# One planner, four edits: when begun projections go on, how value rounds are cut, which head group VectorE's blocks come from, and when a thin value round may start

## The chip, the cores and the metric

The kernel runs on one core of a Trainium2 chip. The metric is device microseconds of that core for one execution, and runs are compared by their median. A core has five engines that the text names as the profile does: TensorE (PE for its matmuls, PEld for its weight loads), VectorE (DVE), ScalarE (ACT), GpSimd (POOL) and SyncE (SP), which here only issues DMAs. Each engine works through its own queue in the order in which the program has it; semaphores tie the queues together.

## The reference

Two attention blocks stand side by side in the output's columns: A, a linear attention, and B, a full softmax attention. Both have S = 2048 rows, D = 512 columns, 32 heads of 16.

```python
# A: x @ wqkv -> q, k, v of 32 heads with 16 columns each
phi = lambda t: jnp.where(t > 0, t + 1, jnp.exp(t)) + 1e-6
pq, pk = phi(q), phi(k)
kv  = jnp.einsum("bhsd,bhse->bhde", pk, v)
z   = jnp.einsum("bhsd->bhd", pk)
num = jnp.einsum("bhqd,bhde->bhqe", pq, kv)
den = jnp.einsum("bhqd,bhd->bhq", pq, z)[..., None] + 1e-6
a   = (num / den) heads joined @ wo
# B: its own x, wqkv, wo
scores = jnp.einsum("bhqd,bhkd->bhqk", q, k) * Dh ** -0.5
p = softmax(scores)
b = einsum("bhqk,bhkd->bhqd", p, v) heads joined @ wo
return jnp.concatenate([a, b], axis=-1)
```

B's cost is its 32 x 2048 x 2048 exponentials.

## The kernel before

**Units and blocks.** B is cut into 32 units: one of four groups of eight heads (Gp), one of four chunks of 512 queries (c), and the even or the odd heads of the group (e_). A unit has 64 blocks: four head groups g (32 rows of the array each) times 16 key tiles j of 128 keys. One block is a matmul "128 keys by 512 queries" from KM and QT into one PSUM bank (`qk`, line 743). 2048 blocks in all.

**Three ways through PSUM.** Of eight banks, five (pS) are ScalarE's, as one slot of three banks and one of two; two (pD) serve VectorE's blocks and, one at a time, every projection and all of A's work; one (pPV) holds the sum of the values.

- ScalarE's blocks: `fill_act_cand` puts three or two score matmuls into the free slot, and line 905 takes the exponential of the whole slot into PT.
- VectorE's blocks: `d_pick` chooses a block for a free pD bank when VectorE's and GpSimd's backlogs are small. Line 839 computes a scaled and shifted integer into DI that, read as float16, is an approximate exponential; two blocks form a group, and line 952 makes two shifted copies of it on GpSimd (DJ). The three tables are used with three weighted copies of V.
- Values: a block of ScalarE's is one matmul with V (17 columns: 16 and a one for the denominator) into its head group's 32 rows of pPV; a block of VectorE's is three. Up to four, one for each head group, stand side by side in a round (line 998). `pv_cand` forms up to two rounds (PVB is 8) of what is ready.

When a unit's 192 or fewer value matmuls are in, VectorE transposes pPV (line 1023), divides (lines 1028 and 1029), and every other unit is transposed back into ON (line 1034). Then pPV is free for the next unit.

**Jobs.** The projections of B (`proj_job`, `v4_job`), all of A (`akv_job`, `akvsum_job`, `aq_job`, `aden_job`, `anum_job`) and the output matmuls (`omm_job`) are jobs with stages: TensorE stages, mostly two halves of the contraction, into one pD bank, then stages on VectorE, ScalarE or a DMA. The bank is taken with the first half and given back after the first read-out.

**The planner.** All instructions are ordered while the program is built: a loop keeps a planned time T for each engine, collects candidates, each with a start, a priority and a duration, and takes among those that could start within 0.03 us of the earliest the one with the lowest priority number. A score fill for ScalarE has 0; later stages of jobs are put into a list by `push` with their job's priority (2 for most, on TensorE); value rounds have 1 when at least 12 value matmuls are outstanding or the unit is at its end, otherwise 4; a block for VectorE alone has 3. Candidates on TensorE that would still run when ScalarE is due for its next fill are left out. Every instruction goes through `Sched.add`, which finds what it must wait for; writes with the same `accum` tag on the same engine don't wait for each other. The order is the planner's, the times are the chip's.

**Filling idle time.** Where the planner leaves TensorE idle for over 0.25 us, `fill_idle` puts in matmuls of zeros (FZ, line 1155): as many as bring TensorE's share of streaming in the last 3.4 us (FW) to 0.7 (FU). `streams` keeps the planned streaming times.

**The lines that the change touches**

```python
        order = sorted(range(4), key=lambda g: (g in used, -len(rem[u][g]), g))
        ...
            if len(rounds[0]) < 4 and not final and len(rd) < 8:
                t_ += PVW
            dur = switch("v") + 0.22 * len(rounds)
        ...
            return t_, dur, run, (1 if out_ >= 12 or final else 4)
```

The first is `choose`, which says which head group's next block is taken: the one with most blocks left. In the second a first round with fewer than four head groups is held back by PVW, 0.5 us, unless eight value matmuls are ready.

Of the kernel before, what the change touches and what calls it, by code (L numbers as in the profile page):

```python
# [21 lines left out]
class Sched:  # L22
# [16 lines left out]
    def add(self, lane, fn, reads=(), writes=(), name="", queue=None,  # L39
            extra_deps=(), accum=None, force_signal=False):  # L40
        if queue is None:
            queue = lane
            assert lane in self.ENGINES, lane
        op = _Op()
        op.idx = len(self.ops)
        op.lane = lane
        op.fn = fn
        op.pos = len(self.lane_ops[lane]) + 1
        op.name = name
        op.queue = queue  # L50
        op.waits = []
        op.sig = force_signal
        op.count = 0
        deps = set(extra_deps)
        for r in reads:
            w = self.last_write.get(r)
            if w is not None:
                deps.add(w)
        for r in writes:
            w = self.last_write.get(r)  # L60
            if w is not None:
                if not (accum is not None and self.acc_tag.get(r) == (lane, accum)):
                    deps.add(w)
            for rd in self.readers.get(r, ()):
                deps.add(rd)
            self.acc_tag[r] = (lane, accum) if accum is not None else None
# [168 lines left out]
def bass_concat_heads__linear_attn_block__softmax_full_mha__prompt_kernel(nc, A_x, A_wqkv, A_wo, B_x, B_wqkv, B_wo, out):  # L235
# [6 lines left out]
    NU = NGP * NC * 2  # L242
# [18 lines left out]
    FU = 0.7  # L261
    LATE = 0.1
    LONE = 0.0
    FW = 3.4
    TRACE = None

# [8 lines left out]
    with es:  # L275
# [160 lines left out]
        class Job:  # L436
# [13 lines left out]
            def stage_done(self, i, end, bk, bi):  # L450
# [6 lines left out]
                if i + 1 < len(self.stages):  # L457
                    eng2, dur, fn = self.stages[i + 1]
                    push(eng2, end if eng2 == eng else vis(eng, end),
                         self.prio if eng2 == "pe" else (0 if eng2 == "act" or (i + 1 <= self.rel and self.bank) else min(self.prio, 2)), dur,  # L460
                         lambda st_, en_, fn=fn: (fn(bk), self.stage_done(i + 1, en_, bk, bi)), getattr(fn, "kind", "f"))
# [241 lines left out]
        pk = ["f"]  # L703

        def switch(kind):
            return 0.0 if pk[0] == kind else 0.1
# [9 lines left out]

        def choose(u, n, used=()):

            got, t0 = [], 0.0
            order = sorted(range(4), key=lambda g: (g in used, -len(rem[u][g]), g))  # L720
            for g in order:
# [64 lines left out]
        def d_pick(at, used):  # L786
# [14 lines left out]
            else:  # L801
                buf = dgroup["buf"]
            ch = choose(u, 1, used)
            if ch is None or not ch[0] or ch[1] > at:
# [3 lines left out]
        def d_take(pk):  # L808
            b, buf, bi = pk
            take([b])  # L810
            dfree[bi] = None
            if not dgroup["open"]:
# [148 lines left out]
        def pv_cand():  # L961
# [20 lines left out]
            while len(rounds) < PVB // 4 and any(byg):  # L982
# [3 lines left out]
                rounds.append(rnd)  # L986
            if len(rounds[0]) < 4 and not final and len(rd) < 8:
                t_ += PVW
            dur = switch("v") + 0.22 * len(rounds)
            def run(st, en):  # L990
                for x in sum(rounds, []):
# [19 lines left out]
                if todo[u] == 0:  # L1011
# [4 lines left out]
                    push("dve", vis("pe", en), -1, 0.63, lambda st_, en_: unit_done(u, en_))  # L1016
            return t_, dur, run, (1 if out_ >= 12 or final else 4)

# [114 lines left out]

        streams = []

        def fill_idle(st, kind):
# [4 lines left out]
            if not gs and bi is None:  # L1141
                return 0
            lo = st - FW
            while streams and streams[0][1] <= lo - 5.0:
                streams.pop(0)
            need = FU * FW - sum(max(0.0, min(y, st) - max(x, lo)) for x, y in streams)
            a += switch("v")
            n = min(int((b - (0.0 if kind == "v" else 0.1) - a) / 0.216), int(need / 0.216 + 0.999))
            if n <= 0:
                return 0  # L1150
            g = gs[0] if gs else 0
            dst = PVb if gs else f32v(DBANK[bi])
# [14 lines left out]
        while True:  # L1167
# [20 lines left out]
            if pc is not None:  # L1188
                opts.append((pc[0], pc[3], "pe", pc[1], pc[2], None, "v"))
            jc = job_cand()  # L1190
# [10 lines left out]
            t0 = min(o[0] for o in opts)  # L1201
            o = min((o for o in opts if o[0] <= t0 + 0.03), key=lambda o: (o[1], o[0]))
            st, _, eng, dur, run_, c_, kind = o
# [101 lines left out]
```

## Time and profile before

| | |
|---|---|
| median of three runs | 765.57 us (763.3 to 768.93) |
| the profiled execution | 767.73 us, its span 765.8 us |
| instructions | 18359 |
| mean granted clock of TensorE | 0.973 |
| HBM read and written | 4.19 MB each, 11 GB/s over the span |

How to read it: a busy time is the union of an engine's instructions, a group's row gives output and inputs by the program's names, the shape, the count, the busy time and the mean of one in ns, and behind the second bar the engine's idle time just before these instructions with what ended it. Line numbers are those of the kernel before.

The stages run into each other, so there are no phases to set apart but the start, some 11.6 us in which inputs land and the first projections are made, and the end, the last 9 us with the last output rows.

```profile
0.81 5.50 DMA xTb<-in_B_x_dram
6.35 1.90 PE pS L476 x16
8.25 2.96 PE pD L476 x31
11.58 46.66 ACT PT L905 x41
```

These are the first pieces of the chain of waits in order of time: start, length, what.

### The profile page before, as it was taken

To read this page: it belongs to the slowest core of one execution; us is meant where nothing else is said; L and a number is where in the kernel's file an instruction comes from. 1 tells how busy PE (TensorE), PEld (TensorE's weight loads), DVE (VectorE), ACT (ScalarE), POOL (GpSimd) and SP (SyncE) were. 2 spreads that over 40 slices of the span, in tenths; PEclk is the share of its full clock that TensorE was granted. 3 is DMA by queue.
4 is the path that set the end of the run, shared out by engine and by line. 5 is a ranking of instruction groups with operands and counts; after the bars stand their busy time and mean duration, and the time that the engine had idled before them with its cause. 6 is when DMAs were issued, how large, how long until landed. Compare 5 with 4: busy or idle time off the path is not lost.

```text
span 765.8 us, 18359 instructions
## 1 busy us (share of the span) xinstructions
PE 696.7 (91%) x7975; PEld 225.5 (29%) x7975; DVE 541.7 (71%) x858; ACT 732.2 (96%) x664; POOL 535.0 (70%) x529
## 2 busy tenths in 40 slices
PE   8899999989899999899999999999998899999886
PEld 4322333333323233322222223322222222222222
DVE  5885868787767767759768746797875866867561
ACT  5999999999989989999999999999999999999995
POOL 4576877567586678745778748776676775869880
PEclk9998999999989979999999899999999999999999
DMA  9400101021011010200210100200100001110000
GB/s 216 116 2 2 28 2 36 12 37 33 2 28 30 2 28 2 63 12 12 49 29 1 36 8 22 55 10 15 29 21 9 1 15 43 29 36 1 15 15 32
DMA packets 54501, 21.68 MB, mean 28 GB/s; under 512 B 45200, under 2 KB 53904, under 8 KB 54416
## 3 DMA queue, kind: packets, MB, share of 16 engines
q1 hardware_dynamic: 53360, 20.20, 11.6%
q8 instruction: 64, 1.05, 0.5%
q10 hardware_dynamic: 1056, 0.26, 0.2%
q14 instruction: 21, 0.17, 0.1%
HBM read 4.19 MB, written 4.19 MB: 11 GB/s over the span
## 4 chain that ended last, share of the span: by engine, by line
ACT 75%; PE 13%; DVE 9%; DMA 1%; POOL 1%; issue 0%; ACTq 0%
ACT PT L905 74%; PE pPV L998 4%; PE pS L743 4%; DVE DI L839 3%; PE pD L476 3%; PE pD L743 2%; ACT EA L590 1%; DVE EA L591 1%; DVE KV L593 1%; DMA xTb<-in_B_x_dram 1%; POOL DJ L952 1%; DVE PQT L593 1%; DVE OT L1023 1%; DVE OT L1029 1%; PE pPV L1155 1%
## 5 line engine op out<-in xcount | busy, mean ns | idle before, releaser
L905 ACT ACTIVATE PT<-pS 128x1536 f16<-128x1536 f32 x627 | 719.3, 1388 | 15.6 <-PE pS L743 9.8
L952 POOL TENSOR_SCALAR DJ<-DI 128x1024 int16<-128x1024 int16 x480 | 511.2, 1065 | 204.8 <-DVE DI L839 174.7
L839 DVE TENSOR_SCALAR DI<-pD 128x512 int16<-128x512 f32 x471 | 318.1, 694 | 108.4 <-PE pD L743 94.8
L743 PE MATMUL pS<-QT,KM 32*128 32x512 bf16 x1568 | 250.8, 393 | 44.3 <-ACT PT L905 37.3
L998 PE MATMUL pPV<-PT,VV 128*17 128x512 f16 x1568 | 253.9, 392 | 0.5 <-ACT PT L905 0.3
L998 PE MATMUL pPV<-DJ,VV 128*17 128x512 f16 x960 | 185.0, 385 | 0.3
L743 PE MATMUL pD<-QT,KM 32*128 32x512 bf16 x480 | 177.2, 393 | 8.5 <-DVE DI L839 5.4
L743 PEld LDWEIGHTS pS<-QT,KM 32*128 32x128 bf16 x1568 | 59.9, 91 | 258.0 <-ACT PT L905 227.9
L998 PE MATMUL pPV<-DI,VV 128*17 128x512 f16 x480 | 102.9, 384 | 3.4 <-DVE OT L1023 2.3
L998 PEld LDWEIGHTS pPV<-PT,VV 128*17 128x17 bf16 x1568 | 56.7, 88 | 74.6 <-issue 66.2
L998 PEld LDWEIGHTS pPV<-DJ,VV 128*17 128x17 bf16 x960 | 42.6, 88 | 47.7 <-issue 35.4
L743 PEld LDWEIGHTS pD<-QT,KM 32*128 32x128 bf16 x480 | 41.7, 91 | 46.5 <-DVE DI L839 26.6
L1023 DVE STREAM_TRANSPOSE OT<-pPV 128x512 f32<-128x512 f32 x32 | 22.8, 712 | 35.3 <-PE pPV L998 35.3
L476 PE MATMUL pD<-Wa,xTa 128*32 128x256 bf16 x1024 | 44.1, 280 | 1.2 <-DVE DI L839 1.0
L1155 PE MATMUL pPV<-FZ 128*17 128x512 bf16 x115 | 43.3, 400 | 0.0
L476 PE MATMUL pD<-xTb,Wb 128*32 128x512 bf16 x496 | 42.1, 393 | 0.9 <-DVE DI L839 0.7
L480 DVE CAST KV<-pD 128x512 bf16<-128x512 f32 x30 | 20.6, 686 | 18.7 <-PE pD L476 18.5
L608 DVE CAST KV<-pD 128x512 bf16<-128x512 f32 x32 | 21.9, 685 | 13.8 <-PE pD L476 13.5
L998 PEld LDWEIGHTS pPV<-DI,VV 128*17 128x17 bf16 x480 | 23.1, 88 | 26.8 <-issue 14.5
L476 PEld LDWEIGHTS pD<-Wa,xTa 128*32 128x32 bf16 x1024 | 27.1, 97 | 11.2 <-DVE DI L839 4.8
L1029 DVE TENSOR_TENSOR OT<-OT,ZR 128x256 bf16<-128x256 f32 x32 | 21.5, 671 | 0.9
L576 POOL TENSOR_SCALAR VV<-VV 128x544 bf16<-128x544 bf16 x24 | 16.6, 690 | 7.2 <-DVE VV L572 6.2
(76 smaller groups left out, 376.2 us busy)
## 6 DMA issues: line engine op xcount, KB each, us to landing
out_dram<-KV SPq DMA_DIRECT2D x32, 128.0 KB, 1.7
KM<-KR SPq DMA_DIRECT2D x96, 16.0 KB, 1.8
Wa<-in_A_wqkv_dram SPq DMA_DIRECT2D x1, 1024.0 KB, 6.6
Wb<-in_B_wqkv_dram SPq DMA_DIRECT2D x2, 384.0 KB, 5.2
Wb<-in_B_wqkv_dram SPq DMA_DIRECT2D x1, 512.0 KB, 4.3
Wa<-in_A_wqkv_dram SPq DMA_DIRECT2D x1, 512.0 KB, 7.3
Wa<-in_A_wo_dram SPq DMA_DIRECT2D x1, 512.0 KB, 6.6
Wb<-in_B_wo_dram SPq DMA_DIRECT2D x1, 512.0 KB, 4.1
```

Source lines behind the costliest of these rows:

```text
L476: ins = e.matmul(out[32 * g:32 * g + 32], lhsT=lhsT[:, 32 * g:32 * g + 32], rhs=rhs, start=start, stop=stop, tile_position=(0, 32 * g))
L480: return lambda e, bk: (e.tensor_copy(out_fn(), in_fn(bk)) if lane == "dve" else e.activation(out_fn(), in_fn(bk), ACTF.Copy))
L576: st.append((lane, 0.25 if lane == "dve" else 0.65, f_op(lane, lambda e, k=k: e.tensor_scalar(vv(k), vv(0), SW[k], 0.0, op0=ALU.mult, op1= ...
L608: st.append(("dve", 0.6, f_ev("dve", lambda e, bk: e.tensor_copy(KV[:, t, 2:514], f32v(bk)), [], [("KV", t)])))
L743: return e.matmul(dst, lhsT=KM[32 * g:32 * g + 32, Gp % 2, e_, j * 128:(j + 1) * 128], rhs=QT[32 * g:32 * g + 32, Gp % 2, c * 512:(c + 1) ...
L839: sch.add("dve", lambda e: e.tensor_scalar(DI[:, buf, i * 512:(i + n) * 512], DB[:, bi * 512:(bi + n) * 512], ESC, EB, op0=ALU.mult, op1=A ...
L905: sch.add("act", lambda e: e.activation(PT[:, row, c0:c0 + w], SCR[sl][:, 0:w], ACTF.Exp, scale=SC), reads=skeys(sl), writes=[("PT", row, ...
L952: sch.add(ln, lambda e: e.tensor_scalar(J, I, 1.0, float(SH[k]), op0=ALU.mult, op1=ALU.add), reads=[("DI", buf, i) for i in range(n)], wri ...
L998: sch.add("pe", lambda e, g=g, j=j, h=h, k=k, P=P, first=first, last_=last_: e.matmul(PVb[32 * g:32 * g + 17, 0:512], lhsT=VV[:, Gp % 2, k ...
L1023: sch.add("dve", lambda e: e.transpose(OT[:, 0, :], PVb[:, 0:512]), reads=[("PV", g) for g in range(4)], writes=[("OT", 0)])
L1029: ("dve", 0.35, f_op("dve", lambda e: e.tensor_tensor(xn[:, :, 16 * e_:16 * e_ + 16], o[:, :, 0:16], zr.unsqueeze(2).broadcast_to([128, 16 ...
L1155: ins = e.matmul(dst[32 * g:32 * g + 17, 0:512], lhsT=FZ[:, 0:17], rhs=FZ[:], start=not gs, stop=not gs, tile_position=(0, 32 * g))
```

## The change

Nothing is computed differently; the planner's choices change, and with them the order of instructions and the number of blocks that go either way.

1. A later TensorE stage of a begun job gets priority 0.9 (`CPRIO`) instead of its job's own.
2. `pv_cand` offers, where it had found two rounds, both the two and the first alone (a tie goes to the longer). Priority 1 begins at 16 outstanding value matmuls (`VHI`) instead of 12.
3. A thin first round is held back only while TensorE's planned streaming in the last 3.4 us is over 0.65 (`UT`); `streaming`, new, computes that share, and `fill_idle` uses it too.
4. For a block of VectorE's, `choose` prefers the head group that has given VectorE the fewest blocks in this unit (`dcnt`, `DBAL`).
5. `fill_idle` may fill between two score fills with zero matmuls in the score matmuls' array mode, into a free pD bank, so that the mode need not change.
6. `Sched.add` takes a list of accumulation tags, one for each write. No call in the kernel passes one.

```diff
+    DBAL = 1
+    CPRIO = 0.9
+    VHI = 16
+    UT = 0.65
...
                     push(eng2, end if eng2 == eng else vis(eng, end),
-                         self.prio if eng2 == "pe" else (...), dur,
+                         (CPRIO if i + 1 else self.prio) if eng2 == "pe" else (...), dur,
...
+        def streaming(t_):
+            lo = t_ - FW
+            while streams and streams[0][1] <= lo - 5.0:
+                streams.pop(0)
+            return sum(max(0.0, min(y, t_) - max(x, lo)) for x, y in streams) / FW
...
-        def choose(u, n, used=()):
+        dcnt = [[0] * 4 for u in range(NU)]
+
+        def choose(u, n, used=(), forD=False):
...
-            order = sorted(range(4), key=lambda g: (g in used, -len(rem[u][g]), g))
+            order = sorted(range(4), key=lambda g: (g in used, dcnt[u][g] if forD and DBAL else 0, -len(rem[u][g]), g))
...
-            ch = choose(u, 1, used)
+            ch = choose(u, 1, used, True)
...
             take([b])
+            dcnt[b[0]][b[2]] += 1
...
-            if len(rounds[0]) < 4 and not final and len(rd) < 8:
+            if len(rounds[0]) < 4 and not final and len(rd) < 8 and streaming(t_) > UT:
                 t_ += PVW
-            dur = switch("v") + 0.22 * len(rounds)
-            def run(st, en):
+            def make(rounds):
+                return switch("v") + 0.22 * len(rounds), lambda st, en: run(st, en, rounds)
+            def run(st, en, rounds):
...
-            return t_, dur, run, (1 if out_ >= 12 or final else 4)
+            pr = 1 if out_ >= VHI or final else 4
+            return [(t_, *make(rounds[:n]), pr) for n in range(len(rounds), 0, -1)]
...
-            need = FU * FW - sum(max(0.0, min(y, st) - max(x, lo)) for x, y in streams)
+            need = (FU - streaming(st)) * FW
+            row = pk[0] == "q" and kind == "q" and bi is not None
...
+            if row:
+                def f(e):
+                    for _ in range(n):
+                        ins = e.matmul(f32v(DBANK[bi]), lhsT=FZ[0:32, 0:128], rhs=FZ[0:32, :], start=True, stop=True, tile_position=(0, 0))
+                    return ins
...
-                opts.append((pc[0], pc[3], "pe", pc[1], pc[2], None, "v"))
+                for q_ in pc:
+                    opts.append((q_[0], q_[3], "pe", q_[1], q_[2], None, "v"))
...
-            o = min((o for o in opts if o[0] <= t0 + 0.03), key=lambda o: (o[1], o[0]))
+            o = min((o for o in opts if o[0] <= t0 + 0.03), key=lambda o: (o[1], o[0], -o[3]))
```

More of the change, by code (lines that the diff above doesn't have):

```diff
@@ L58, in add @@
                 deps.add(w)
-        for r in writes:
+        for k_, r in enumerate(writes):
+            tag = accum[k_] if isinstance(accum, list) else accum
             w = self.last_write.get(r)
             if w is not None:
-                if not (accum is not None and self.acc_tag.get(r) == (lane, accum)):
+                if not (tag is not None and self.acc_tag.get(r) == (lane, tag)):
                     deps.add(w)
@@ L65, in add @@
                 deps.add(rd)
-            self.acc_tag[r] = (lane, accum) if accum is not None else None
+            self.acc_tag[r] = (lane, tag) if tag is not None else None
         if lane not in self.ENGINES and self.lane_ops[lane]:
@@ L459, in stage_done @@
                     push(eng2, end if eng2 == eng else vis(eng, end),
-                         self.prio if eng2 == "pe" else (0 if eng2 == "act" or (i + 1 <= self.rel and self.bank) else min(self.prio, 2)), dur,
+                         (CPRIO if i + 1 else self.prio) if eng2 == "pe" else (0 if eng2 == "act" or (i + 1 <= self.rel and self.bank) else min(self.prio, 2)), dur,
                          lambda st_, en_, fn=fn: (fn(bk), self.stage_done(i + 1, en_, bk, bi)), getattr(fn, "kind", "f"))
@@ L703, in bass_concat_heads__linear_attn_block__softmax_full_mha__prompt_kernel @@
         pk = ["f"]
+        streams = []
+        def streaming(t_):
[3 more added lines that the diff above has]
+            return sum(max(0.0, min(y, t_) - max(x, lo)) for x, y in streams) / FW
         def switch(kind):
@@ L1132, in job_cand @@
             return best
-        streams = []
         def fill_idle(st, kind):
@@ L1142, in fill_idle @@
                 return 0
-            lo = st - FW
-            while streams and streams[0][1] <= lo - 5.0:
-                streams.pop(0)
-            need = FU * FW - sum(max(0.0, min(y, st) - max(x, lo)) for x, y in streams)
-            a += switch("v")
-            n = min(int((b - (0.0 if kind == "v" else 0.1) - a) / 0.216), int(need / 0.216 + 0.999))
+            need = (FU - streaming(st)) * FW
+            row = pk[0] == "q" and kind == "q" and bi is not None
+            fk = "q" if row else "v"
+            a += switch(fk)
+            n = min(int((b - (0.0 if kind == fk else 0.1) - a) / 0.216), int(need / 0.216 + 0.999))
             if n <= 0:
                 return 0
+            if row:
[3 more added lines that the diff above has]
+                    return ins
+                sch.add("pe", f, reads=["FZ"], writes=[DBANK[bi][3]])
+                for i in range(n):
+                    streams.append((a + 0.216 * i, a + 0.216 * (i + 1)))
+                return n
             g = gs[0] if gs else 0
```

## The prediction

> **What bounds the kernel now.** I read the page first (busy shares, the row of the clock, the chain of waits by engine and line), then the groups by shape, the waits, the chain in order of time, and the windows around the stretches where the clock is low.
>
> ```profile
> span 765.8 us, 18359 instructions
> PE 696.7 (91%) x7975; PEld 225.5 (29%) x7975; DVE 541.7 (71%) x858; ACT 732.2 (96%) x664; POOL 535.0 (70%) x529
> PEclk9998999999989979999999899999999999999999
> ACT 75%; PE 13%; DVE 9%; DMA 1%; POOL 1%; issue 0%; ACTq 0%
> ...
> L905 ACT ACTIVATE PT<-pS 128x1536 f16<-128x1536 f32 x314 | 502.6, 1601 | 13.3 <-PE pS L743 7.9 <-PE pD L743 4.9 <-issue 0.2
> L905 ACT ACTIVATE PT<-pS 128x1024 f16<-128x1024 f32 x313 | 367.9, 1175 | 2.3 <-PE pS L743 1.9
> ```
>
> ScalarE (ACT) is busy 96% of the span and holds 75% of the chain; what it does is 627 exponentials, 314 over three score blocks and 313 over two: 1568 of the 2048 blocks. The other 480 go through VectorE and GpSimd. TensorE's 91% is modelled; what tells about it is who waits for whom:
>
> ```profile
> PEld pS L743 <- ACT PT L905: 227.9, 464, 1.2
> POOL DJ L952 <- DVE DI L839: 174.7, 104, 7.5
> PEld pPV L998 <- issue: 116.2, 487, 0.8
> DVE DI L839 <- PE pD L743: 94.8, 146, 2.5
> ...
> PEld pPV L998 <- POOL DJ L952: 6.8, 20, 0.6
> ```
>
> 464 of the 627 score fills stand ready and wait for ScalarE to free a slot, 227.9 us together, 0.49 us each: TensorE has that much room. VectorE has blocks to wait for (94.8 us), and GpSimd waits for VectorE (174.7 us). So the time is: when ScalarE starts, its exponentials one behind the other, its idle time between them, and a tail.
>
> ```profile
> 299.08 18.08 ACT PT L905 x16
> ...
> 11.60:757.00 745.40, 683.70 (x7823) 218.28 (x7822) 536.63 (x848) 728.87 (x659) 527.58 (x504) 0.97 0.11 25
> 58.40:65.20 6.80, 6.80 (x52) 1.50 (x50) 2.84 (x5) 5.37 (x5) 5.24 (x6) 0.50 0.00 0
> 222.20:229.10 6.90, 6.90 (x49) 1.73 (x45) 3.29 (x6) 5.42 (x5) 6.34 (x8) 0.51 0.00 0
> 266.60:276.90 10.30, 10.30 (x77) 3.33 (x76) 5.00 (x9) 7.07 (x7) 8.10 (x8) 0.50 0.00 0
> 369.00:372.40 3.40, 3.40 (x22) 0.86 (x19) 2.97 (x5) 3.24 (x4) 2.59 (x3) 0.50 0.00 0
> 433.90:444.10 10.20, 10.09 (x49) 2.02 (x46) 5.35 (x8) 7.11 (x7) 8.14 (x8) 0.50 0.07 14
> 621.60:625.00 3.40, 3.40 (x23) 0.65 (x27) 2.16 (x5) 3.25 (x4) 3.16 (x4) 0.50 0.00 0
> ```
>
> From the chain: in a clean stretch 16 exponentials (40 blocks) take 18.08 us, overlapped, so 1.13 us each and 0.452 us per block; the 1601 and 1175 ns of one are not the pace. From the windows (length, then busy times; ACT is the fourth, the clock stands behind POOL's): from the first exponential to the last, 745.40 us, ScalarE is idle 745.40 - 728.87 = 16.5 us. In the six stretches with the clock at half, 41.0 us, it is idle 1.43 + 1.48 + 3.23 + 0.16 + 3.09 + 0.15 = 9.5 us; in the 704.4 us that remain, 7.0 us.
>
> **The change, part by part.**
>
> *The split of the blocks.* The order in which instructions stand is planned while the program is built, so what the edits do to it can be counted in the two programs. New: 309 exponentials over three blocks, 309 over two and one over one, 1546 blocks; 502 blocks on VectorE. That comes from two edits: the second half of a begun projection now runs ahead of value rounds (priority 0.9 for 2), so its pD bank, one of two, is free sooner for a block of VectorE's; and VectorE's blocks are dealt evenly over the four head groups, so 32 instead of 9 of its instructions take both banks at once. 22 blocks fewer on ScalarE by 0.452 us: **-9.9 us**, all on the path.
>
> What the 22 blocks cost elsewhere:
>
> ```profile
> L952 POOL TENSOR_SCALAR DJ<-DI 128x1024 int16<-128x1024 int16 x480 | 511.2, 1065 | 204.8 <-DVE DI L839 174.7 <-DVE BN L548 1.3
> L839 DVE TENSOR_SCALAR DI<-pD 128x512 int16<-128x512 f32 x462 | 307.1, 684 | 102.0 <-PE pD L743 92.9 <-PE pS L743 3.6 <-PE pD L476 2.1
> L839 DVE TENSOR_SCALAR DI<-pD 128x1024 int16<-128x1024 f32 x9 | 11.0, 1219 | 6.4 <-PE pS L743 4.5 <-PE pD L743 1.8
> 205.03 0.39 PE L998 MATMUL pPV<-DI,VV 128*17 128x512 f16 x4
> 205.25 0.60 PE L998 MATMUL pPV<-DJ,VV 128*17 128x512 f16 x8
> ```
>
> GpSimd: 22 more shifts by 1.065 = 23.4 us, against 765.8 - 535.0 = 231 us idle, most of it waiting for VectorE. VectorE: 24 single conversions fewer (-16.4 us), 23 double ones more (+28.0): +11.6 us against 224 idle. TensorE: 44 more value matmuls and 16 more of the zero matmuls that fill idle time (145 for 129). Four side by side pass in 0.22 us (the rows: x4 at 205.03, the next at 205.25), so between 3 us if rounds stay full and 13 us if each stands alone; ScalarE would feel neither while fills have 0.49 us to spare. Counting passes over both programs in order, a round of up to four as one pass of 0.22 us, gives 482 us before and 484 after: rounds are fuller, and the extra is hidden. If that cover went, 3 us is the price. I book +0.3 us: the 7.0 us of scattered idle grow with the blocks of VectorE, 22 in 480.
>
> *Score fills that come too late.* In two places of the old order both fills stand together, with both of ScalarE's slots already empty:
>
> ```profile
> 276.26 3.72 ACT L905 ACTIVATE PT<-pS 128x1536 f16<-128x1536 f32 x3 [1.89 <-PE pD L743]
> ...
> 441.31 1.03 PE L743 MATMUL pS<-QT,KM 32*128 32x512 bf16 x5
> 441.96 2.37 ACT L905 ACTIVATE PT<-pS 128x1536 f16<-128x1536 f32 x2 [3.03 <-PE pS L743]
> ```
>
> They cost 1.89 and 3.03 us. Such a pair of fills stands three times in the old order (the first is the start) and once, at the start, in the new. Both lie in half-clock stretches, so they are part of the 9.5 us.
>
> *Value rounds in pieces, and thin ones at once.* Each candidate of two rounds is now offered as two or one, so it fits between score fills; a round with fewer than four groups is held back 0.5 us only if TensorE was streaming over 0.65 of the last 3.4 us. This moves no work off ScalarE; it evens TensorE's load, and that matters because of what stands ahead of a half-clock stretch:
>
> ```profile
> 218.80:222.20 3.40, 2.10 (x28) 0.74 (x28) 3.37 (x5) 3.25 (x4) 2.10 (x3) 1.00 0.32 72
> 263.20:266.60 3.40, 2.22 (x21) 0.59 (x17) 3.40 (x5) 2.90 (x3) 2.35 (x3) 1.00 0.02 5
> 430.50:433.90 3.40, 2.79 (x36) 1.27 (x36) 2.24 (x5) 3.40 (x4) 3.20 (x4) 1.00 0.00 0
> 618.20:621.60 3.40, 2.88 (x22) 0.77 (x20) 3.04 (x7) 3.40 (x4) 3.18 (x4) 1.00 0.21 43
> ```
>
> The 3.4 us ahead of these show TensorE at 62 to 85%, where the span's mean is 91%; the stretches themselves last 3.4 us or two or three times that. So a poorly filled 3.4 us is followed by half clock, and it takes no pause: TensorE was busy 2.10 us or more in each. I set the passes of three successive fills against ScalarE's time for their three exponentials (3.4 us): 48 of some 620 such stretches are filled under half in the old order, 25 in the new; over their full time, so that TensorE itself sets the pace, is 13.9 us of work in the old, 9.9 in the new. Bounds for the idle in half clock: all 9.5 us go, or it grows by half (+4.8) if the low stretches that are left are those that count. I take half, **-4.8 us**, by the counts and by the two dry places, which are gone and alone are 4.9.
>
> The Trainium skill (TensorE: Matmul & The Clock Gate, "Why this matters for your kernels") says to leave no idle gap over some 3 us between bursts, since a window of idle brings the half clock back. The rows above differ: the clock fell after windows with 2 us and more of busy time, so the measurement decides. By the rule thin rounds would buy nothing here, and the sum would be the 9.9 us alone (the second rival).
>
> *Changes of mode.* Score matmuls sit in row groups, value matmuls and projections in column groups, and the 116.2 us over 487 times is the 0.24 us that a value round stands behind a score fill for no profiled reason. Pieces could have multiplied this. The count of changes in either direction falls from 1242 to 1224, so nothing is added; 18 by 0.24 is 4 us of TensorE's room, booked at nothing. The Trainium skill (TensorEngine Tiling (Array Packing), "Key Properties") says that changing the tiling mode drains TensorE, which would speak against pieces; the trace's 0.24 us agrees that a change costs, the count says there are fewer.
>
> **The sum.** The profiled execution took 767.7 us with a span of 765.8; the median of the three runs is 765.57 (763.3 to 768.93), 2.2 less than it, which I put down to less half-clock idle, so its half is (9.5 - 2.2) / 2 = 3.7. 765.6 - 9.9 - 3.7 + 0.3 = **752.3 us**.
>
> **The rivals.** *(a) The forecast*, 746 to 758. 0.62.
> *(b) Only the exponents pay.* Half clock comes as often as before, at other places, and the dry places are replaced by others: 765.6 - 9.9 + 0.3 = 756.0, up to 761 with half again as much. For it: the stretches depend on details that the planned times don't hold, and the old order was planned to keep TensorE filled too. Against: the two counts. 0.22.
> *(c) Half clock all but vanishes*: all 9.5 - 2.2 = 7.3 us and some of the 7.0 go: 744 to 746. 25 low stretches are left, so 0.08.
> *(d) TensorE is held at a value round, slower.* TensorE takes its queue in order. Pieces stand closer behind the shifts of GpSimd that they read, and GpSimd has 23 us more to do; behind a waiting piece stands the next score fill, and ScalarE for that. A wait is free up to the 0.49 us that a fill has; one group of shifts late (two by 1.065 = 2.13 us) costs 2.13 - 0.49 = 1.64. At 11 late groups of 251 the 18 us are there that make it 1% slower than before; at 20 it is 752.3 + 33 = 785. For it: the page's row of GpSimd in 40 slices has three at 8 tenths or more near the end.
>
> ```profile
> POOL 4576877567586678745778748776676775869880
> ```
>
> Against: such waits come to 6.8 us over 20 times now, 0.34 each, under the 0.49. 0.06.
> That the change does nothing is out: 22 blocks have moved in the built program. The last 0.02 is for a time between (b) and (d).
>
> **The chances.** Under 757.9 us is over 1% faster (about what can be told here from no change): all of (c), nearly all of (a), and a fifth of (b): 0.08 + 0.60 + 0.05 = 0.73. Within 1%: 0.02 + 0.17 + 0.02 = 0.21. Slower, over 773.2: 0.06. The range 745 to 761 leaves out (d), the last 0.02, and a part of (c) and of (b), a sixth in all.
>
> **What would show it.** In the profile after: 618 exponentials on line 905's successor at 1.13 us; ScalarE's idle time between first and last near 12 us for 16.5; two to four half-clock stretches for six; no ScalarE wait over 1.5 us; "pPV <- POOL DJ" still under 10 us. (d) would show as that last wait growing past 25 us and ScalarE waits for pS beside it. I am wrong if the pace is not 1.13, which would mean that more work on VectorE or GpSimd slows ScalarE, or if half clock grows.

## The result, and the profile after

The changed kernel takes 757.18 us, the median of eight runs (753.79 to 759.63); the kernel before takes 768.27 over eight runs (763.3 to 774.11). The ratio is 0.9858, with a 95% interval of 0.9816 to 0.9900: 11 us or 1.4% faster. The profiled execution took 759.52 us with a span of 757.8.

From the page of the changed kernel: the span, the busy shares, the clock in 40 slices, the chain of waits by engine.

```profile
span 757.8 us, 18489 instructions
PE 685.8 (91%) x8035; PEld 220.5 (29%) x8035; DVE 558.9 (74%) x857; ACT 724.6 (96%) x656; POOL 558.1 (74%) x551
PEclk9999999999999999999899899999999999999899
ACT 57%; PE 18%; DVE 17%; POOL 5%; issue 1%; SPq 1%; DMA 1%; DVEq 0%
```

ScalarE is busy 96% as before, and yet it holds 57% of the chain where it held 75%. VectorE's share has gone from 9 to 17%, GpSimd's from 1 to 5%.

The groups by shape and the waits of the changed kernel:

```profile
L921 ACT ACTIVATE PT<-pS 128x1536 f16<-128x1536 f32 x309 | 484.8, 1569 | 11.6 <-PE pS L758 7.4 <-PE pD L758 3.3
L921 ACT ACTIVATE PT<-pS 128x1024 f16<-128x1024 f32 x309 | 352.2, 1140 | 4.7 <-PE pS L758 2.4 <-PE pD L758 1.7
L855 DVE TENSOR_SCALAR DI<-pD 128x512 int16<-128x512 f32 x438 | 289.5, 683 | 88.2 <-PE pD L758 79.5 <-PE pS L758 5.0
L855 DVE TENSOR_SCALAR DI<-pD 128x1024 int16<-128x1024 f32 x32 | 39.1, 1222 | 25.8 <-PE pD L758 18.2 <-PE pS L758 7.7
...
PEld pS L758 <- ACT PT L921: 203.0, 408, 1.1
POOL DJ L968 <- DVE DI L855: 143.8, 97, 5.1
PEld pPV L1015 <- POOL DJ L968: 12.9, 29, 1.4
ACT PT L921 <- PE pS L758: 9.8, 19, 1.4
PE pPV L1015 <- POOL DJ L968: 3.5, 7, 0.9
```

The split is as counted. The room of TensorE has shrunk: 408 fills wait for ScalarE, not 464, and value rounds wait for GpSimd's shifts 16.4 us (the rows with 12.9 and 3.5) instead of 6.8. VectorE's busy time rose by 17.2 us (541.7 to 558.9).

The windows: each kernel from its first exponential to its last (the first row is of the kernel before, the second of the changed one), then the changed kernel's five stretches at half clock.

```profile
11.60:755.30 743.70, 682.04 (x7813) 217.71 (x7812) 535.47 (x845) 728.87 (x659) 527.58 (x504) 0.97 0.11 25
```
```profile
9.40:747.10 737.70, 673.27 (x7875) 213.25 (x7874) 552.68 (x844) 721.35 (x651) 550.70 (x526) 0.98 0.11 26
...
200.70:204.10 3.40, 3.28 (x27) 0.59 (x27) 1.45 (x4) 1.81 (x2) 0.34 (x1) 0.50 0.00 0
361.10:368.00 6.90, 6.46 (x47) 1.71 (x50) 5.84 (x10) 5.62 (x6) 4.19 (x4) 0.51 0.21 42
429.40:436.20 6.80, 6.80 (x50) 1.42 (x50) 4.52 (x8) 5.63 (x5) 5.36 (x6) 0.50 0.00 0
613.70:617.10 3.40, 3.40 (x21) 0.70 (x19) 1.70 (x4) 3.40 (x4) 2.61 (x3) 0.51 0.00 0
702.50:709.30 6.80, 6.80 (x50) 1.33 (x47) 3.33 (x5) 5.44 (x5) 5.38 (x6) 0.50 0.01 2
```

The stretch of the exponentials is only 6.0 us shorter, although 9.9 us of them are gone. (The prediction's window of the kernel before ended at 757.0, 1.7 us after the last exponential; ended at it, ScalarE's idle time there is 14.8 us and not 16.5.) What ScalarE loses can be worked out: the stretch, less 0.452 us for each block and 16.3 us for the 32 exponentials of the linear block (0.51 each). Before: 743.7 - 1568 x 0.452 - 16.3 = 18.7 us. After: 737.7 - 1546 x 0.452 - 16.3 = 22.6 us. Put down exponential by exponential to the half-clock stretches and the rest, it is 10.8 and 7.8 us before, 7.3 and 15.2 after. The parts come from one profiled execution each, and where an exponential lies across the edge of a stretch its place is a choice that moves them by 1 to 2 us. So half clock cost less, as forecast, and a loss that the forecast raised by only 0.3 us doubled. (The start, 11.6 us here and 9.4 there, lies between 9.2 and 11.8 in the profiles of all the kernels below and follows no kernel.)

Every run records the granted clock, and 2 x (1 - clock) x span is the time at half clock. Over 35 runs of the kernel before it averages 46 us (24 to 65), over the eight of the changed kernel 18 us (8 to 29). Within the kernel before a run is 0.30 us longer for each us at half clock (correlation 0.96), within the changed one 0.26 (0.97). Both lines end at the same place: with no half clock, spans of 752 and 751 us. By these numbers nearly the whole gain is the half clock, and the 9.9 us of exponentials have vanished. (This is a correlation: it doesn't tell how far half clock makes a run longer, and how far what leaves TensorE waiting brings both.) The experiments are about where they went.

### The profile page after: what moved, and what is told of

Its sections match the earlier page's. It is cut to its first block, busy times and chain, and to the rows that moved or that the text cites. A ratio compares the mean times of both kernels' runs of the same rounds, so it can differ in the third digit from the quotient of the medians.

```text
span 757.8 us, 18489 instructions
## 1 busy us (share of the span) xinstructions
PE 685.8 (91%) x8035; PEld 220.5 (29%) x8035; DVE 558.9 (74%) x857; ACT 724.6 (96%) x656; POOL 558.1 (74%) x551
## 4 chain that ended last, share of the span: by engine, by line
ACT 57%; PE 18%; DVE 17%; POOL 5%; issue 1%; SPq 1%; DMA 1%; DVEq 0%
ACT PT L921 56%; PE pPV L1015 6%; DVE DI L855 6%; PE pS L758 5%; POOL DJ L968 5%; PE pD L481 5%; DVE PQT L598 2%; DVE KV L598 2%; DVE EA L596 2%; ACT EA L595 1%; PE pD L758 1%; DVE OT L1041 1%; DVE OT L1047 1%; SPq L357 1%; DMA Wb<-in_B_wqkv_dram 1%
## 5 line engine op out<-in xcount | busy, mean ns | idle before, releaser
L921 ACT ACTIVATE PT<-pS 128x1536 f16<-128x1536 f32 x619 | 711.7, 1353 | 16.2 <-PE pS L758 9.8
L968 POOL TENSOR_SCALAR DJ<-DI 128x1024 int16<-128x1024 int16 x502 | 535.5, 1067 | 174.7 <-DVE DI L855 143.8
L855 DVE TENSOR_SCALAR DI<-pD 128x512 int16<-128x512 f32 (+1 forms) x470 | 328.6, 720 | 114.0 <-PE pD L758 97.7
L1015 PE MATMUL pPV<-PT,VV 128*17 128x512 f16 x1546 | 247.9, 386 | 0.4 <-ACT PT L921 0.2
L1015 PE MATMUL pPV<-DJ,VV 128*17 128x512 f16 x1004 | 179.1, 392 | 3.8 <-POOL DJ L968 3.5
L758 PE MATMUL pD<-QT,KM 32*128 32x512 bf16 x502 | 172.2, 388 | 7.7 <-DVE DI L855 3.8
L1015 PE MATMUL pPV<-DI,VV 128*17 128x512 f16 x502 | 108.7, 399 | 3.0 <-DVE OT L1041 2.1
L481 PE MATMUL pD<-xTb,Wb 128*32 128x512 bf16 x496 | 37.3, 382 | 2.9 <-DVE DI L855 2.3
L613 DVE CAST KV<-pD 128x512 bf16<-128x512 f32 x32 | 22.0, 687 | 16.7 <-PE pD L481 16.7
L481 PEld LDWEIGHTS pD<-Wa,xTa 128*32 128x32 bf16 x1024 | 22.6, 96 | 15.7 <-issue 7.3
L481 PE MATMUL pD<-xTa,Wa 128*32 128x512 bf16 x256 | 21.0, 383 | 1.4 <-DVE QT L518 0.8
```

The source lines that it names most:

```text
L481: ins = e.matmul(out[32 * g:32 * g + 32], lhsT=lhsT[:, 32 * g:32 * g + 32], rhs=rhs, start=start, stop=stop, tile_position=(0, 32 * g))
L613: st.append(("dve", 0.6, f_ev("dve", lambda e, bk: e.tensor_copy(KV[:, t, 2:514], f32v(bk)), [], [("KV", t)])))
L758: return e.matmul(dst, lhsT=KM[32 * g:32 * g + 32, Gp % 2, e_, j * 128:(j + 1) * 128], rhs=QT[32 * g:32 * g + 32, Gp % 2, c * 512:(c + 1) ...
L855: sch.add("dve", lambda e: e.tensor_scalar(DI[:, buf, i * 512:(i + n) * 512], DB[:, bi * 512:(bi + n) * 512], ESC, EB, op0=ALU.mult, op1=A ...
L921: sch.add("act", lambda e: e.activation(PT[:, row, c0:c0 + w], SCR[sl][:, 0:w], ACTF.Exp, scale=SC), reads=skeys(sl), writes=[("PT", row, ...
L968: sch.add(ln, lambda e: e.tensor_scalar(J, I, 1.0, float(SH[k]), op0=ALU.mult, op1=ALU.add), reads=[("DI", buf, i) for i in range(n)], wri ...
```

## The experiments

Two theories at the start. **A**: the split of the blocks pays, 0.452 us for each block taken off ScalarE. **B**: the filling of TensorE pays, through the clock. Later **C**: VectorE runs later than the planner thinks, each block more on it makes it later, and ScalarE waits for that. A difference is against the kernel before, run on the same chip, so kernels from different chips are compared by their ratios and not by their medians. The last column but one is of the profiled execution, the last one the average over the runs. The blocks are those of the profiles; where a unit gave VectorE an odd number, the expectations, which counted GpSimd's shifts, are 1 or 2 too high (492, 494 and 466 for 490, 493 and 465).

| kernel | blocks on VectorE | us, median | ratio to before (95%) | loss outside half clock, us | half clock, us |
|---|---|---|---|---|---|
| before | 480 | 767.7 (35 runs) | 1 | 7.8 | 46 |
| changed | 502 | 757.2 | 0.986 (0.982 to 0.990) | 15.2 | 18 |
| no pieces | 490 | 762.2 | 0.995 (0.992 to 0.998) | 12.0 | 29 |
| thin rounds held | 498 | 768.1 | 1.002 (0.998 to 1.005) | 15.2 | 48 |
| thin rounds alone | 480 | 762.2 | 0.994 (0.991 to 0.997) | 8.9 | 30 |
| begun jobs alone | 493 | 767.5 | 1.000 (0.997 to 1.003) | 13.4 | 36 |
| no zeros | 502 | 761.9 | 0.995 (0.992 to 0.997) | 11.0 | 58 |
| at most 15 a unit | 465 | 768.6 | 1.004 (1.001 to 1.007) | 8.6 | 20 |
| changed, light VectorE | 502 | 745.6 | 0.975 (0.972 to 0.979) | 6.2 | 16 |
| before, light VectorE | 480 | 757.4 | 0.988 (0.985 to 0.991) | 3.7 | 24 |
| true times | 478 | 754.7 | 0.983 (0.980 to 0.986) | 1.7 | 27 |
| no even dealing | 502 | 765.7 | 0.998 (0.995 to 1.000) | 15.8 | 36 |
| begun jobs as before | 500 | 754.9 | 0.983 (0.980 to 0.987) | 10.1 | 30 |
| phi in one VectorE pass | 498 | 754.2 | 0.981 (0.977 to 0.985) | 5.3 | 34 |

**One edit undone, one edit alone.** No pieces:

```diff
-            return [(t_, *make(rounds[:n]), pr) for n in range(len(rounds), 0, -1)]
+            return [(t_, *make(rounds[:n]), pr) for n in range(len(rounds), len(rounds) - 1, -1)]
```

> The changed kernel, but value rounds are offered only as the longest piece, as before the change. Counted in the built program: 492 blocks on VectorE (502 in the changed kernel, 480 before), 55 weakly filled stretches of TensorE (25, 48), 19.5 us of overfull ones (9.9, 13.9), no pair of late score fills. Theory A, only the split of the blocks pays, 0.452 us per block taken from ScalarE: 12 blocks, 5.4 us under the kernel before (-0.7%). Theory B, filling TensorE evenly pays as well: the stretches are as bad as before, so no more than 5.4 us, and rather 2 to 4, and half clock as long as before (some 40 us, against 27 in the changed kernel). If pieces were a cost (value pieces that wait on GpSimd with a score fill behind them), this kernel would be the faster one, at -12 us or more, with the waits of pPV for DJ back under 8 us.

Measured 762.2 us, -4.1 by the ratio. Within what either allowed, though half clock averages 29 us and not the 40 of theory B; pieces are no cost, without them 7 of the 11 us are gone.

Thin rounds held back as before the change (`UT = -1.0` for 0.65):

> The changed kernel, but thin value rounds are always held back 0.5 us, as before the change. Counted: 498 blocks on VectorE, 49 weakly filled stretches, three pairs of late score fills counting the start (one in the changed kernel). Theory A: 18 blocks by 0.452, -8.1 us against the kernel before (-1.1%). Theory B: -8.1 us at best, and the two late pairs show as waits of ScalarE of 1.5 us and more; half clock near 40 us. If thin rounds at once were a cost (they take TensorE's passes half used), this kernel would be the faster one, under -12 us.

Measured 768.1 us, no gain at all, where both theories had up to 8.1. Theory A falls here: 18 blocks have left ScalarE, and nothing came of it. Half clock averages 48 us.

The kernel before with that edit alone (the other four off, but for the rule for ties):

> The kernel before, with one edit of the change alone: a thin value round is held back only where TensorE streamed over 0.65 of the last 3.4 us. Counted: 480 blocks on VectorE as before, 42 weakly filled stretches for 48, 9.3 us of overfull ones for 13.9, no late pair but the start. Theory A: no block moves, so 0 us. Theory B: the late pairs (4.9 us in the profile of before) are gone and half clock gets a little shorter: -3 to -6 us (-0.4 to -0.8%).

Measured -4.8 us. No block has moved; half clock is 16 us shorter, which by 0.30 is 4.8, and the loss outside it stays near 8 to 9. That fits theory B.

The kernel before with begun jobs first alone:

> The kernel before, with one edit alone: later stages of begun jobs have priority 0.9. Counted: 494 blocks on VectorE (480 before), 51 weakly filled stretches, one late pair besides the start (two before). Theory A: 14 blocks by 0.452, -6.3 us (-0.8%). Theory B: the same, since the filling of TensorE is as before, less some 2 us for the late pair that is gone: -6 to -8 us.

Measured 0 us, a miss for both. The chain of this kernel shows what neither had:

```profile
ACT 63%; PE 19%; DVE 15%; POOL 1%; DMA 1%; issue 1%; DVEq 0%; ACTq 0%
...
11.50:758.20 746.70, 686.50 (x7869) 214.71 (x7867) 548.36 (x854) 725.46 (x654) 539.80 (x518) 0.97 0.11 25
```

Its stretch is 746.7 us with 13 blocks fewer on ScalarE, 3 us longer than the one before; some of that is half clock, 51 us in this execution, the longest of the twelve, for 41 in the one before. VectorE holds 15% of its chain. In the first six rows of the table the loss outside half clock goes with the blocks on VectorE: 8 to 9 us at 480, 12 to 13 at 490 and 493, 15 at 498 and 502. That is theory C. Of the rows below not all follow it: 10.1 at 500, 8.6 at 465.

**The clock and the split, apart.** No zeros:

```diff
-    FU = 0.7
+    FU = 0.0
```

> The changed kernel, planned without the matmuls of zeros that fill TensorE's idle time (FU 0 for 0.7). Counted: 502 blocks on VectorE as in the changed kernel, 75 weakly filled stretches (25 there, 48 before). Theory B, filling decides through the clock: over the runs so far half clock lasts 18 us on average in the changed kernel and 46 us in the one before, and a run of the kernel before is 0.3 us longer for each us of it, so some 75 to 80 us of half clock here and about 7 us more than the kernel before (+0.9%), 16 to 18 more than the changed one. If only long pauses brought the half clock, or the zeros cost TensorE time that score fills need, this kernel would stand at -11 us or under.

Measured -4.1 us by the ratio: 7 us over the changed kernel, not 16 to 18. Half clock averages 58 us, short of the 75 that the count of weak stretches gave. In the profile it is 52 us, and ScalarE loses 23.6 - 11.0 = 12.6 us in it, 0.24 each, near the 0.3; but the loss outside is 4 us smaller, so the total came out low. So half clock rises without the filling, and the time with it. Why the loss outside fell is not shown: the zeros may cost TensorE time, and the order moved too (25 double conversions for 32).

At most 15 blocks of a unit to VectorE:

```diff
+            if sum(dcnt[u]) >= 15:
+                return None
             ch = choose(u, 1, used, True)
```

> The changed kernel with at most 15 blocks of a unit given to VectorE: 466 blocks, 36 fewer than in the changed kernel and 14 fewer than before; 40 weakly filled stretches. Theory A, the split pays 0.452 us per block: 16 us slower than the changed kernel, so +5 us against the kernel before, and up to +10 with the half clock of 40 stretches. Theory C, VectorE runs later than planned and each block more on it brings back some 0.35 us as waits of ScalarE: ScalarE's idle time outside half clock falls from 15 to 5 us, and the time is -4 to 0 us against the kernel before.

Measured +2.8 us, 14 over the changed kernel: between the two. Half clock is as short as in the changed kernel, so the split can be read nearly by itself: 37 blocks more on ScalarE are 16.7 us of work, and the loss outside half clock in the profile is 6.6 us smaller. That leaves 10 us by the profile and 14 by the times, these give or take 4: the split pays, but perhaps 60 to 80% of its price.

The same orders with a lighter VectorE (of the linear block's phi and of the two maxima 64 columns instead of 512; the linear half of the output is left out by it):

```diff
-                e.tensor_reduce(QMX[:, i:i + 1], QT[:, r, cs], axis=AX.X, ...)
+                e.tensor_reduce(QMX[:, i:i + 1], QT[:, r, sc * 512:sc * 512 + 64], axis=AX.X, ...)
...
-                e.tensor_scalar(EA[:, q, :], EA[:, q, :], 1.0, 1e-6, ...)
+                e.tensor_scalar(EA[:, q, 0:64], EA[:, q, 0:64], 1.0, 1e-6, ...)
```

> The changed kernel, every instruction in its place, but VectorE's passes over the linear block's exponentials (the two of phi) and the two kinds of maxima for the overflow guard cover 64 columns instead of 512; the linear half of the output is not computed by it. VectorE has some 55 us less to do, the other engines the same. Theory C: ScalarE's idle time outside half clock falls from 15 us to 5 to 7, so 8 to 10 us under the changed kernel and -19 to -21 us against the kernel before. Rival, TensorE's own order brings the waits: as the changed kernel, -11 us.

> The kernel before with the same cut of VectorE's work (the linear half of the output is not computed by it). Theory C: its idle time outside half clock is 8 us and falls to some 5: -2 to -4 us. So the changed kernel would lead by 16 to 18 us between the two light kernels, for 11 between the full ones: that is what the split of the blocks is worth where VectorE keeps up. Rival: 0 us here, and the lead stays 11 us.

Measured -18.9 us for the changed kernel, close to what C had, and its loss outside half clock fell from 15.2 to 6.2 us, although VectorE's busy time fell by 34 us (558.9 to 524.8) and not 55. TensorE has the same instructions in the same order. Adding all rows of the waits of TensorE, it waits for VectorE 82 us in the kernel before, 98 in the changed one, 57 and 52 in the light changed and the light one before. For GpSimd it waits 19.6 us in the changed kernel and still 17.9 in the light one, so the loss that went was VectorE's, hardly GpSimd's.

The kernel before came to -9.1 us, far more than the 2 to 4 expected, and the lead, expected at 16 to 18, stayed at 10 to 12: a miss for C. The two last columns say where: here half clock fell, from 41 us on this chip to 24, by 0.3 some 5 us, and the other loss by 4.1. The light kernels have 16 and 24 us of half clock; that is 2.4 us of their lead, and 7 to 9 remain, with some 3 us of uncertainty, for the 9.9 us of the split. So where VectorE keeps up the split comes near its full price; that the rest is noise is not shown. A heavier VectorE costs by the clock as well, since with the same order half clock is longer; that this is TensorE standing still for VectorE is the likely way, and was not tested.

From the page of the light kernel before, same order as the kernel before, the chain and the clock:

```profile
PEclk9999999999989999999999799999999999999999
ACT 90%; PE 7%; DVE 1%; DMA 1%; POOL 0%; issue 0%; ACTq 0%
```

VectorE has all but gone from the chain, 1% for 9%.

**The planner told the truth.** In the code a conversion of one block is planned at 0.09 + 0.51 = 0.60 us; the rows above have 683 ns. The passes of the linear block are planned at 0.2 and 0.6, the division's product at 0.35.

```profile
L1047 DVE TENSOR_TENSOR OT<-OT,ZR 128x256 bf16<-128x256 f32 x32 | 25.0, 781 | 1.0
...
L598 DVE SCALAR_TENSOR_TENSOR PQT<-PQT,EA 128x512 bf16<-128x512 bf16 x16 | 18.5, 1157 | 0.2
L598 DVE SCALAR_TENSOR_TENSOR KV<-KV,EA 128x512 bf16<-128x512 bf16 x16 | 18.1, 1130 | 0.4
L596 DVE TENSOR_SCALAR EA<-EA 128x512 bf16<-128x512 bf16 x32 | 17.7, 554 | 3.6 <-ACT EA L595 3.5
```

They take 0.55, 1.13 to 1.16, and 0.78. The edit, of which four places are shown; the read-outs, the maxima, the transpose of pPV and GpSimd's shifts got their measured times as well:

```diff
-                push("dve", vis("pe", en), 0, 0.09 + 0.51 * n, p1)
+                push("dve", vis("pe", en), 0, 0.15 + 0.535 * n, p1)
...
-                ("dve", 0.2, f_op("dve", lambda e: e.tensor_scalar(EA[:, q, :], ...
+                ("dve", 0.55, f_op("dve", lambda e: e.tensor_scalar(EA[:, q, :], ...
...
-                ("dve", 0.6, f_op("dve", lambda e: e.scalar_tensor_tensor(x, x, 0.0, E, ...
+                ("dve", 1.1, f_op("dve", lambda e: e.scalar_tensor_tensor(x, x, 0.0, E, ...
...
-                  ("dve", 0.35, f_op("dve", lambda e: e.tensor_tensor(xn[...
+                  ("dve", 0.75, f_op("dve", lambda e: e.tensor_tensor(xn[...
```

> The changed kernel, but the planner is told the durations that the profile shows for VectorE (0.685 us for a conversion instead of 0.60, 0.69 for read-outs, 0.71 for the transpose of pPV, 0.55, 1.1 and 0.75 for the passes that take long beside GpSimd) and for GpSimd's shifts (1.07 for 1.01). It then gives VectorE 478 blocks (502 in the changed kernel, 480 before), and 54 weakly filled stretches are counted. If ScalarE's idle time comes from VectorE running late: idle time outside half clock at 5 us or less (15 in the changed kernel), half clock under 30 us although the count of weak stretches is as high as before, and 758 to 761 us, -7 to -10 us against the kernel before. If the planned filling of TensorE decides half clock: over 45 us of it, and the time of the kernel before.

Measured 754.7 us, -13 by the ratio, better than the 7 to 10 expected. From its page, its windows and its waits:

```profile
span 753.3 us, 18373 instructions
PEclk9999999999999999999999999999999979999899
ACT 92%; PE 5%; DMA 1%; SPq 1%; DVE 0%; issue 0%
...
9.30:743.20 733.90, 656.77 (x7822) 207.02 (x7821) 541.57 (x844) 727.80 (x660) 524.70 (x502) 0.98 0.11 26
PEld pS L758 <- ACT PT L921: 289.4, 548, 1.2
PEld pPV L1015 <- POOL DJ L968: 3.8, 15, 0.6
ACT PT L921 <- PE pS L758: 3.5, 7, 0.7
```

ScalarE has 24 blocks more than in the changed kernel, and its stretch is 3.8 us shorter. It loses 733.9 - 1570 x 0.452 - 16.3 = 8 us in all, 1.7 outside half clock. VectorE is not on the chain, 548 of the fills stand ready, and TensorE waits for VectorE 37 us instead of 98. The conversions and shifts are as long as before on the chip (685 and 1064 ns); only the plan now expects them so. But the plan also gave 24 blocks back to ScalarE, 10.8 us, so over the changed kernel the gain is 2 us, with overlapping intervals. The true times were not tried on the kernel before. And half clock is 27 us with 54 weakly filled stretches counted, where 48 of them went with 46 us before: the count of planned passes does not foretell it, probably because what leaves TensorE idle on the chip is not in the plan.

**The other two edits undone.** Without even dealing (`DBAL = 0`), and with a begun job's own priority:

```diff
-                         (CPRIO if i + 1 else self.prio) if eng2 == "pe" else (...), dur,
+                         self.prio if eng2 == "pe" else (...), dur,
```

> The changed kernel, but VectorE's blocks are taken from the head group with most blocks left, as before the change. Counted: 502 blocks on VectorE as in the changed kernel, 36 weakly filled stretches (25), 13 double conversions (32), 13.1 us of overfull stretches (9.9). VectorE has 19 double conversions fewer, which are 38 single ones, 0.15 us each more: 3 us more work on it. Between the changed kernel and 3 to 4 us above it: -7 to -11 us against the kernel before.

> The changed kernel, but later stages of begun jobs have their job's own priority, as before the change. Counted: 500 blocks on VectorE, 31 weakly filled stretches, 9 double conversions. That edit alone brought nothing; if the edits add up, this kernel is as fast as the changed one, -11 us. If going on first pays only together with the others, by freeing banks for pairs of VectorE's blocks: -6 to -9 us.

Without even dealing 765.7 us: 9 of the 11 us are gone, a miss, with the same 502 blocks. Half clock is 18 us longer, some 5 us by 0.3; the loss outside it is about the same (15.8 us for 15.2), with longer single waits of ScalarE (3.4 us for its own score matmuls, 2.7 for a score matmul of VectorE's). With a begun job's own priority the kernel is as fast as the changed one, with overlapping intervals: no effect of that edit shows in either direction.

Undone singly, pieces, thin rounds and even dealing take 7, 11 and 9 us away, far more than the 11 that all bring, so the edits don't add up. Each of these kernels is also a new order of the whole program, and how much two orders differ by chance was not measured.

**A faster version.** phi in two passes, ScalarE's exponential and one of VectorE's:

```diff
-                e.activation(E, x, ACTF.Exp)
-                e.tensor_scalar(EA[:, q, :], EA[:, q, :], 1.0, 1e-6, op0=ALU.min, op1=ALU.add)
-                e.scalar_tensor_tensor(x, x, 0.0, E, op0=ALU.max, op1=ALU.add)
+                e.activation(E, x, ACTF.Exp, scale=1.0 / EUL)
+                e.scalar_tensor_tensor(x, E, EUL, x, op0=ALU.min, op1=ALU.max)
...
-                e.tensor_copy(PQT[:, 0, bq, :], f32v(bk))
+                e.tensor_scalar(PQT[:, 0, bq, :], f32v(bk), EUL, EUL, op0=ALU.mult, op1=ALU.add)
```

> A try at a faster version: the changed kernel with less work for VectorE in the linear block. phi, times the constant e, which cancels between numerator and denominator, is max(min(exp(x + 1), e), e x + e); e x + e is made in the read-out from PSUM, ScalarE's exponential takes the scale 1/e, and one pass of VectorE follows instead of two. The 1e-6 of phi, far under the rounding of its type, is left out. 32 passes fall (17.7 us in the profile of the changed kernel), and 32 read-outs become two of half the width (0.14 us more each, 4.5 us). Counted: 498 blocks on VectorE, 27 weakly filled stretches. From the two light kernels 0.2 us of time for each us taken off VectorE: 2 to 3 us under the changed kernel, less 4 blocks by 0.45 = 1.8: -11 to -13 us against the kernel before. If the waits are TensorE's own: -9 us.

Measured -14.7 us by the ratio, the lowest of the full kernels here, though its interval overlaps those of the two at 0.983 and that of the changed kernel. The loss outside half clock fell to 5.3 us; half clock is longer than in the changed kernel, 34 us. True times and this together were not run.

## Why the prediction came out right, point by point

The time and the sign were right, 13.3 us forecast and 11.1 measured. That is partly luck: one term was missing, another was half its size, and the two errors nearly cancel. The time itself, 752.3 us, was 4.9 low, 2.7 of it because the kernel before stands at 768.3 over eight runs and not at the 765.6 of three.

- *The split, -9.9 us.* As work it is right: 618 exponentials, and the pace held (34 of them in 38.6 us, 1.13 each). As time it is not: *"What the 22 blocks cost elsewhere"* is the step that failed. It set VectorE's 11.6 us more against 224 us idle and booked 0.3 us. VectorE's busy time rose by 17.2 us, its longer passes included, and the idle time stood at other places than the need: the loss outside half clock rose by 7.4 us (one profile each, as said), and the light kernels and the true times show that VectorE, behind its planned times, makes most of it.

```profile
12.13 38.60 ACT PT L921 x34
```

- *Half clock, -3.7 us* was too small, and is the larger part of the gain if the correlation is taken as cause: 46 us against 18, at 0.26 to 0.30, is 7 to 8.5 us. The forecast halved the cost of one profile of the kernel before. Its reason, evener planned passes, fits the thin rounds alone, and fails as a measure: three kernels with 48 to 54 weak stretches have 24 to 46 us. Nor is a poorly filled 3.4 us always followed by half clock, as the prediction read from the stretches that were: laid out from the start of the first half-clock stretch in steps of 3.41 us, the trace of the kernel before has 30 more windows in which TensorE was busy at most 85% of the time, down to 60%, and the clock stayed full in the next one.
- Together: -9.9 + 7.4 - 8 is -10.5.
- *Late pairs of fills, gone:* no wait of ScalarE for a score fill is over 1.4 us, as foretold. Half-clock stretches: five, not two to four. ScalarE's idle time between its first and last exponential was to fall to 12 us; it is 16.4, and 14.8 in the kernel before: this sign pointed at the missing term.
- *Rival (d), value rounds held by GpSimd:* the sign that was named, that wait under 10 us, failed at 16.4, short of the 25 that were to show the rival. In the light kernel these waits stay and the loss goes, so GpSimd was hardly what cost the time. (The prediction's 11 late groups give 752.3 + 18 = 770.3 us, not yet its 773.2; it takes 13.)
- *Rival (b), only the exponentials pay, at 756 us,* is refuted by the thin rounds held: 18 blocks fewer on ScalarE, half clock as before, and 768 us.
- *Changes of mode:* "pPV <- issue" fell from 116.2 to 94.9 us and "pS <- issue" rose from 23.9 to 40.7, together 4 us less. In the true times "pS <- issue" is 9.0, so it goes with fills that come late; it was not tested as a cost of its own.

What stays open: why even dealing is worth 9 us with the same blocks, how much of these differences is the chance of one order against another, how far half clock is a cause and how far a companion of late work, and why the loss outside it is smaller without the zeros.

## What to carry to other kernels

Where the order is planned with written durations, compare them with the profile's before adding work to an engine: a queue in order passes an engine's delay on to all others, and 25% idle time on average is no cover. Here the true times, added to the edits, took the loss outside half clock from 15.2 us to 1.7, though by giving blocks back the plan was only some 2 us faster, within the noise. When a kernel's runs scatter, plot them over the granted clock first; it tells how much of a gain goes with the clock.

## What was not expected of the hardware

VectorE's instructions that take two operands from SBUF, and phi's TENSOR_SCALAR from SBUF to SBUF, are longer while GpSimd runs. From the timeline of the kernel before (start, length):

```profile
208.04 0.27 DVE L591 TENSOR_SCALAR EA<-EA 128x512 bf16<-128x512 bf16 x1
208.20 2.49 POOL L952 TENSOR_SCALAR DJ<-DI 128x1024 int16<-128x1024 int16 x2 [2.27 <-DVE DI L839]
208.35 1.44 DVE L593 SCALAR_TENSOR_TENSOR KV<-KV,EA 128x512 bf16<-128x512 bf16 x1
209.71 0.68 DVE L839 TENSOR_SCALAR DI<-pD 128x512 int16<-128x512 f32 x1
```

The pass that lies mostly before GpSimd's start takes 0.27 us, 0.55 on average in the changed kernel; the one within its two shifts 1.44, where the same pass takes 0.69 with GpSimd idle, and the two shifts take 2.49 for 2.13. The conversion from PSUM takes 0.68 either way. The Trainium skill (GPSIMD Engine Reference, section 1, Specifications) says that GpSimd shares its SBUF interfaces with VectorE and contends with instructions of two SBUF inputs or in a two-port mode; the trace agrees for the instructions of two inputs, with these numbers; in which mode the TENSOR_SCALAR runs it doesn't show. So VectorE's work has no fixed length: the four groups above took 71.4 us in the kernel before and take 79.3 in the changed one. The number of shifts doesn't decide it, for the true times with 478 blocks have 78.4; it must be which passes meet a shift.

And half clock is no fixed trait of an order: the same order of TensorE's, on the same chip, had 41 us of it or 24, by VectorE's load alone.
